# Loading order, weight pieces and paired start-up steps in an attention plus SmeLU kernel

## The chip, the cores and the metric

The kernel runs on one core of a Trainium2 chip. The metric is device time in microseconds. Before the change it is 308.18 us, the median of three runs (307.83 to 308.30). The profiled run took 307.91 us, and its trace spans 306.1 us from the first to the last instruction. A core has a matrix engine (PE, with its weight load PEld), a vector engine (DVE), a scalar engine (ACT), a GpSimd engine (POOL), and a SyncE engine (SP). Sixteen DMA engines move the data. POOL here mainly issues loads, [...].

## The reference: what is computed

```python
# attention: 8 batches, 8 heads, 576 positions, head size 64
scores = q @ k.T / sqrt(64)              # kept only where |i - j| <= 32
attn   = softmax(scores)
x      = (attn @ v)  ->  [8*576 = 4608 tokens, 8*64 = 512 features]
# feed-forward block
h = x @ w_in                             # w_in: 512 x 2048
g = h        if h >= 1                   # SmeLU with beta = 1
    0        if h <= -1
    (h+1)**2 / 4   otherwise
out = g @ w_out                          # w_out: 2048 x 512
```

All inputs and the output are float32 in DRAM. The kernel computes with bfloat16 operands and float32 sums.

## The kernel before

The work on the tokens goes in blocks of 256 (`TB`). For each block there are eight slots, one for each 256 of the 2048 hidden columns: `a = 8*t + f`. A slot projects (`project`: eight matmuls of 256 columns, two halves `j` by four 128-row groups `kk` of `w_in`), applies SmeLU, and leaves its result in `gT`. The products with `w_out` follow some slots later (`pair` for the first 512 tokens, `unit` after that). The attention of the next batch is spread between the slots. For the first batch there is nothing to hide it behind, so the start of the kernel is a hand-written prelude, and then slots 0 to 5 with the rest of batch 0's attention between them.

The order of the loads on POOL at the start (q of the first half goes by SP and ACT):

```python
def load_w_in(c0, c1, h):            # 64 partitions, 4 row groups, c1 - c0 columns
    nc.gpsimd.dma_start(out=w_in[64 * h:64 * h + 64, :, c0:c1],
                        in_=moe_w_in.rearrange("(h y d) f -> h d y f", h=2, d=64)[h][:, :, c0:c1])

# k of the first half (2 loads) ... then
load_v(0, 0)
P.affine_select(out=step, ...)       # for the identity and the mask
for n in range(1, 4):
    load_v(0, n)
...
cuts = [0, 256, 512, 768, 1024, 1280, 1792, DFF]
w = [(load_w_in, c0, c1, h) for c0, c1 in zip(cuts, cuts[1:]) for h in range(2)]
put(w[:4] + [(load_half, 1, t, h) for t in range(2) for h in range(2)] + w[4:12])   # load_half: rest of q, k
put([(load_w_out, 0, 0, 4)] + w[12:])
put([(load_w_out, 0, k, k + 4) for k in range(4, 16, 4)] + [(load_rows, 1, t) for t in range(2)])
put([(load_v, 1, n) for n in range(4)])
```

The prelude ends with the sums of the first 256 tokens (`sums` multiplies the exponentials with v and with ones; its `end` runs Ln and Exp on ACT, and `flush` later multiplies on DVE into `xT`). Then the rest of batch 0 hangs on slots 1 to 5:

```python
    scores(0, (1, 2), (0, 2), (0, 2), None, ps_p)
    keep_warm(4, ps_h, "hp")         # matmuls on zeros
    e0 = sums(0, 0, 0, TB)
    e1 = sums(0, 1, 0, TB, ps_p)
    keep_warm(5, ps_h, "hp")
    e0()
    e1()
# ...
pairs = [(6, 0), (7, 1), (8, 2), (9, 3), (11, 4), ...]          # (slot, pair of w_out)
two_on_act = (1, 7, 8, 9, 10, 11, 12)
at(1, (tposes, 0, (0, 1), (1, 1)))                               # rest of q and k transposed
at(2, (scores, 0, (0, 1), (0, 2), (2, 4)), (scores8, 0, ps_o))
at(3, (scores, 0, (1, 2), (0, 2), (2, 4), ps_n), (sums, 0, 0, TB, MAIN, ps_s))
at(4, (sums, 0, 1, TB, MAIN))
at(5, (sums, 0, 0, MAIN, S, ps_s))
```

In the slot loop (cut to what the change touches):

```python
for a in range(NF * NB + 2 * NF):
    # ...
    if a in (0,):                     # slots 0 and 1 are projected together
        hps = [ps_h.tile([128, 2, TB], FP, name="hp", tag="hp") for _ in range(2)]
        for y in range(2):
            for n in range(2):
                project(hps[n], f + n, r0, [(j, y + 2 * m) for j in range(2) for m in range(2)], y == 0, y == 1)
    elif not hps:
        # ps_o for slot 6, else ps_h
        hps = [pool.tile([128, 2, TB], FP, name="hp", tag=tag)]
        project(hps[0], f, r0, [(j, kk) for j in range(2) for kk in (0, 2, 1, 3)], True, True)
    hp = hps.pop(0)
    rr = ewp.tile([128, 2, TB], FP, name="rr")
    A.activation(rr, hp, AF.Relu, scale=0.5, bias=0.5)
    mx = ewp.tile([128, 2, TB], FP, name="mx")
    if a in two_on_act:
        A.activation(mx, rr, AF.Square)
        V.scalar_tensor_tensor(g, hp, 1.0, mx, op0=ALU.max, op1=ALU.min)
    else:
        V.tensor_max(mx, hp, rr)
        V.scalar_tensor_tensor(g, rr, 1.0, mx, op0=ALU.min, op1=ALU.mult)
    flush(); run(a)                  # the attention that hangs on this slot
    for x in post: ...               # pair or unit: products with w_out
```

Of the kernel before, what the change touches and what calls it, by code (L numbers as in the profile page):

```python
# [7 lines left out]
FP = mybir.dt.float32  # L8
# [6 lines left out]
def kernel(  # L15
# [30 lines left out]
    LONG = 2  # L46

# [7 lines left out]
    ps_h = ctx.enter_context(tc.tile_pool(name="ps_h", bufs=2, space=bass.MemoryType.PSUM))  # L55
# [25 lines left out]
    def load_half(half, t, h, eng=None, x=None):  # L81

        src, dst, nm = ((q, qn, "qh"), (k, kn, "kh"))[t]
        if (0, half) not in dst:
            dst[0, half] = early.tile([128, 2, S], BF, name=nm, tag=nm, bufs=2) if x is None else x
        (eng or nc.gpsimd).dma_start(out=dst[0, half][:, h], in_=src[0].rearrange(  # L86
            "(h y) (l p j) d -> h l p y (j d)", h=2, l=2, p=32)[h][half])
# [22 lines left out]
    def load_w_in(c0, c1, h):  # L110
        nc.gpsimd.dma_start(out=w_in[64 * h:64 * h + 64, :, c0:c1],  # L111
                            in_=moe_w_in.rearrange("(h y d) f -> h d y f", h=2, d=64)[h][:, :, c0:c1])
# [19 lines left out]
    load_v(0, 0)  # L132
    P.affine_select(out=step, in_=step, compare_op=ALU.is_ge, fill=-1.0, base=-65, channel_multiplier=-1,
                    pattern=[[1, 257]])
    for n in range(1, 4):
        load_v(0, n)
# [7 lines left out]
    def put(todo):  # L144
        for fn, *x in todo:
            fn(*x)

    cuts = [0, 256, 512, 768, 1024, 1280, 1792, DFF]
    w = [(load_w_in, c0, c1, h) for c0, c1 in zip(cuts, cuts[1:]) for h in range(2)]
    put(w[:4] + [(load_half, 1, t, h) for t in range(2) for h in range(2)] + w[4:12])  # L150
    put([(load_w_out, 0, 0, 4)] + w[12:])
    put([(load_w_out, 0, k, k + 4) for k in range(4, 16, 4)] + [(load_rows, 1, t) for t in range(2)])
# [60 lines left out]
    def scores(b, ys, pars, cs, eng, pool=ps_s, w=128, ready=None):  # L213

        if b not in pt:
            pt[b] = ptp.tile([128, 2, 2, 2, 512], BF, name="pt")
        ps = ready or two_banks(pool)
        n = 0
        if eng is None and not ready:
            cols = (ys[1] - ys[0]) * (pars[1] - pars[0]) * (cs[1] - cs[0])  # L220
            add_mask([ps[:, h] for h in range(2)], cols, w)
        for y1 in range(*ys):
            for par in range(*pars):
                for c2 in range(*cs):
                    c = 2 * c2 + par
                    for a in range(2):
                        for h in range(2):
                            s0 = S * (y1 + 2 * a) + 64 * c
                            nc.tensor.matmul(ps[HD[a], h, w * n:w * n + w], kT[b][HD[h], s0:s0 + 64],  # L229
                                             qTs[b % 3][HD[h], PAD + s0 - 32:PAD + s0 - 32 + w],  # L230
                                             start=eng is not None, stop=True, skip_group_check=True)
                    n += 1
        p = pt[b][:, :, ys[0]:ys[1], pars[0]:pars[1], 128 * cs[0]:128 * cs[1] - 128 + w]
        m = 2 if n > cs[1] - cs[0] else 1
        p = p[:, :, ys[0] - ys[0]] if ys[1] - ys[0] == 1 else p[:, :, :, 0]
        like = "p h (y j) -> p h y j"
        A.activation(p, ps[:, :, :w * n].rearrange(like, y=m), AF.Exp, scale=D ** -0.5)  # L237
        mask(eng, p, mask4[:, :256 * n].rearrange("p (h j) -> p h j", h=2).rearrange(like, y=m))

    def scores8(b, eng, pool=None):  # L240

        p = pt8[b] = ptp.tile([128, 2, 2, TAIL], BF, name="pt8")
        if pool:
            ps = [pool.tile([128, 2 * TAIL], FP, name="s8", tag="op") for h in range(2)]
        else:
            bb = two_banks(ps_s)
            ps = [bb[:, h, :2 * TAIL] for h in range(2)]
# [9 lines left out]
        like = "p h y j -> p h (y j)"  # L257
        if pool:
            for h in range(2):
                A.activation(p[:, h].rearrange("p y j -> p (y j)"), ps[h], AF.Exp, scale=D ** -0.5)  # L260
        else:
            A.activation(p.rearrange(like), bb[:, :, :2 * TAIL], AF.Exp, scale=D ** -0.5)
# [4 lines left out]
    def sums(b, y1, lo, hi, pool=ps_n):  # L267
# [3 lines left out]
        todo = []  # L271
        if lo < MAIN:
            ys, D0 = (y1,), w
            for par in range(2):
                a0 = max(lo, 32 * par)
                off = 32 - 64 * par
                todo.append((None, a0 - lo, hi - lo, lambda a, h, par=par, a0=a0, off=off: (
                    pt[b][HD[a], h, y1, par, a0 + off:hi + off])))
                for c2 in range(4):
                    q0, q1 = max(0, 128 * c2 - off, lo), min(128 * c2 + 128 - off, hi)  # L280
                    if q0 < q1:
                        todo.append((NC * y1 + 2 * c2 + par, q0 - lo, q1 - lo, lambda a, h, par=par, q0=q0, q1=q1, off=off: (
                            pt[b][HD[a], h, y1, par, q0 + off:q1 + off])))
# [36 lines left out]
    def tp1(pool):  # L320
        if pool is ps_h:
            return pool.tile([128, 8, 128], BF, name="tp", tag="hp")
        return pool.tile([128, 2, 8, 128], BF, name="tp", tag="bb")[:, 0]

    def tposes(b, *sets):

        todo = []
        for (t, half), pool in zip(sets, (ps_s, ps_n)):
            tp = pool.tile([128, 2, 8, 128], BF, name="tp", tag="bb")
# [4 lines left out]
    def keep_warm(n, pool, tag):  # L334

        z = pool.tile([128, 512], FP, name="z", tag=tag)
        for _ in range(n):
            nc.tensor.matmul(z, warm[:, :128], warm, start=True, stop=True)
# [9 lines left out]
    with tc.tile_pool(name="ps_p", bufs=1, space=bass.MemoryType.PSUM) as ps_p:  # L348
        keep_warm(11, ps_h, "hp")
# [6 lines left out]
        qq = [tpose(0, n, 0, (A.copy, V.tensor_copy)[n], tp1(ps_h)) for n in range(2)]  # L356
        for x in qq:
            x()
        kk = [tpose(0, n, 1, (A.copy, V.tensor_copy)[n], tp1((ps_n, ps_p)[n])) for n in range(2)]
        keep_warm(1, ps_h, "hp")  # L360
# [5 lines left out]
        scores(0, (0, 2), (0, 1), (2, 3), None, ps_n, 32)  # L366
        scores(0, (1, 2), (0, 2), (0, 2), None, ps_p)
        keep_warm(4, ps_h, "hp")
        e0 = sums(0, 0, 0, TB)
        e1 = sums(0, 1, 0, TB, ps_p)  # L370
        keep_warm(5, ps_h, "hp")
        e0()
        e1()
    ps_o = ctx.enter_context(tc.tile_pool(name="ps_o", bufs=2, space=bass.MemoryType.PSUM))

# [3 lines left out]
    pairs = [(6, 0), (7, 1), (8, 2), (9, 3), (11, 4), (12, 5), (15, 6), (15, 8), (16, 7), (17, 9)]  # L381
    two_on_act = (1, 7, 8, 9, 10, 11, 12)
# [13 lines left out]

    at(1, (tposes, 0, (0, 1), (1, 1)))
    at(2, (scores, 0, (0, 1), (0, 2), (2, 4)), (scores8, 0, ps_o))
    at(3, (scores, 0, (1, 2), (0, 2), (2, 4), ps_n), (sums, 0, 0, TB, MAIN, ps_s))
    at(4, (sums, 0, 1, TB, MAIN))  # L400
    at(5, (sums, 0, 0, MAIN, S, ps_s))
# [29 lines left out]
    def unit(x):  # L431

        tt, j = divmod(x, 16)
        if tt == NT // 128 - 1:
            half, n = divmod(j, 8)
            if n == 0:
                op[tt] = ps_o.tile([128, 256], FP, name="op", tag="op")
# [9 lines left out]
        if j == 0:  # L447
            op[tt] = ps_o.tile([128, DM], FP, name="op", tag="op")
# [7 lines left out]
    def pair(x):  # L456

        half, p, g = x // 8, x % 8 // 4, x % 4
        if (half, p) not in op:
            op[half, p] = ps_o.tile([128, 2, 256], FP, name="op", tag="op"), []  # L460
# [12 lines left out]
    def run(pos):  # L473
        todo = []
        for fn, *x in ev.get(pos, []):
# [4 lines left out]
            else:  # L480
                pool = (x.pop(),) if x[-1] in (ps_s, ps_n, ps_o) else ()
# [11 lines left out]
    hps = []  # L493
    done = 4 * (40 - NF)
    for a in range(NF * NB + 2 * NF):
# [9 lines left out]
        if a == 0 or a > 3:  # L505
            flush()
        if a < NF * NB:
            if wide:
# [3 lines left out]
                hp = ps_h.tile([128, 2, TB], FP, name="hp", tag="hp")  # L512
                for n, kk in enumerate((0, 2, 1, 3)):
# [3 lines left out]
            else:  # L517
                t, f = divmod(a, NF)
                r0 = TB * t % RING
                if a in (0,):  # L520
                    hps = [ps_h.tile([128, 2, TB], FP, name="hp", tag="hp") for _ in range(2)]
                    for y in range(2):
                        for n in range(2):
                            project(hps[n], f + n, r0, [(j, y + 2 * m) for j in range(2) for m in range(2)], y == 0, y == 1)
                elif not hps:
                    pool, tag = (ps_o, "op") if a == 6 else (ps_h, "hp")
                    hps = [pool.tile([128, 2, TB], FP, name="hp", tag=tag)]
                    project(hps[0], f, r0, [(j, kk) for j in range(2) for kk in (0, 2, 1, 3)], True, True)
                hp = hps.pop(0)
                g = gT[:, 2 * f:2 * f + 2, home(t)]  # L530

            rr = ewp.tile([128, 2, TB], FP, name="rr")
            A.activation(rr, hp, AF.Relu, scale=0.5, bias=0.5)  # L533
            mx = ewp.tile([128, 2, TB], FP, name="mx")
            if a in two_on_act:
                A.activation(mx, rr, AF.Square)
                V.scalar_tensor_tensor(g, hp, 1.0, mx, op0=ALU.max, op1=ALU.min)
            else:
                V.tensor_max(mx, hp, rr)  # L539
                V.scalar_tensor_tensor(g, rr, 1.0, mx, op0=ALU.min, op1=ALU.mult)  # L540
# [46 lines left out]
```

The softmax here doesn't subtract the row's maximum and nothing guards it: scores larger than these inputs give would overflow.

## Time and profile before

| engine | busy us | share of 306.1 us | instructions |
|---|---|---|---|
| PE | 298.4 | 97% | 3388 |
| DVE | 239.6 | 78% | 376 |
| ACT | 191.2 | 62% | 320 |
| POOL | 77.1 | 25% | 92 |

The chain of work that ended last is 91% PE, 3% POOL and 2% DMA. Some durations that matter later: a 512-column Relu on ACT takes 595 ns on average, `tensor_max` over 512 columns on DVE 689 ns, `scalar_tensor_tensor` 692 ns, a 1024-column Exp on ACT about 1.0 us. Eight matmuls of 256 columns that follow each other without a gap take 0.87 us on PE.

How to read it: a time line gives start, length, engine, source line, operation, tiles, and how many instructions were merged. What stands in brackets at its end is the idle time just before, with what ended it. Because PE is busy almost without a break, the end moves only if PE starts its dense work earlier or later, or if gaps in it open or close.

### The profile page before, as it was taken

How to read it: one execution, taken by the hardware profiler on the slowest of the kernel's cores; microseconds unless marked ns; L12 is line 12 of the kernel's file. 1: busy time of each engine (PE TensorE's matmuls, PEld its weight loads, DVE VectorE, ACT ScalarE, POOL GpSimd, SP SyncE). 2: the span in 40 equal slices, each digit the busy share in tenths (PEclk: the TensorE clock that was granted, in tenths of full speed). 3: DMA queues.
4: the chain of work that ended last, by engine and by line, in shares of the span. 5: the costliest groups of instructions: out<-in, count | busy, mean ns of one | idle time of the engine just before them, and what ended most of it. 6: DMA issues, size and time to landing. Idle time of an engine off the chain costs nothing.

```text
span 306.1 us, 7974 instructions
## 1 busy us (share of the span) xinstructions
PE 298.4 (97%) x3388; PEld 181.2 (59%) x3388; DVE 239.6 (78%) x376; ACT 191.2 (62%) x320; POOL 77.1 (25%) x92
## 2 busy tenths in 40 slices
PE   8889999999999999999999999999999999999995
PEld 3468878876666676666654544444445444446644
DVE  3268568888888989998999998888888888788700
ACT  3688896748856856776766766665667654444311
POOL 8787661037009009004600900000000000000000
PEclk9999999999999999999999999999999999999999
DMA  9999999999999999999998991550101000000121
GB/s 153 184 197 198 186 196 153 173 156 164 139 186 109 181 169 124 165 144 116 148 127 166 145 156 39 111 115 34 36 34 37 36 34 35 36 34 34 59 80 69
DMA packets 137171, 35.67 MB, mean 117 GB/s; under 512 B 122160, under 2 KB 132912, under 8 KB 137136
## 3 DMA queue, kind: packets, MB, share of 16 engines
q0 software_dynamic: 102976, 18.06, 83.5%
q1 hardware_dynamic: 34016, 16.81, 26.1%
q8 instruction: 26, 0.43, 0.6%
q10 hardware_dynamic: 144, 0.29, 0.3%
q14 instruction: 9, 0.07, 0.1%
HBM read 36.70 MB, written 9.44 MB: 151 GB/s over the span
## 4 chain that ended last, share of the span: by engine, by line
PE 91%; POOL 3%; DMA 2%; ACT 1%; issue 1%; DVE 0%; POOLq 0%; ACTq 0%
PE op L449 36%; PE hp L489 22%; PE hp L514 18%; PE bb L295 6%; PE op L464 4%; PE bb L229 2%; DMA w_in<-in_moe_w_in_dram 2%; POOL vn L107 1%; PE op L440 1%; POOL w_in L111 1%; PE tp L189 1%; ACT pt L237 1%; POOL kh L86 1%; POOL qh L86 0%; PE bb L208 0%
## 5 line engine op out<-in xcount | busy, mean ns | idle before, releaser
L533 ACT ACTIVATE rr<-hp 128x512 f32<-128x512 f32 x144 | 85.5, 595 | 86.1 <-PE hp L514 41.7
L449 PE MATMUL op<-w_out,gT 128*128 128x512 bf16 x496 | 126.9, 380 | 0.0
L539 DVE TENSOR_TENSOR mx<-hp,rr 128x512 f32<-128x512 f32 x137 | 94.4, 689 | 26.1 <-ACT rr L533 24.3
L540 DVE SCALAR_TENSOR_TENSOR gT<-rr,mx 128x512 bf16<-128x512 f32 x137 | 94.8, 692 | 4.7
L489 PE MATMUL hp<-xT,w_in 128*128 128x256 bf16 x640 | 83.1, 273 | 2.2 <-DMA w_in<-in_moe_w_in_dram 1.4
L489 PEld LDWEIGHTS <-w_in 128*128 128x128 bf16 x640 | 61.8, 98 | 22.7 <-issue 2.8
L449 PEld LDWEIGHTS <-gT 128*128 128x128 bf16 x496 | 46.1, 98 | 45.2
L514 PE MATMUL hp<-xT,w_in 128*128 128x512 bf16 x256 | 65.7, 379 | 0.0
L514 PEld LDWEIGHTS <-w_in 128*128 128x128 bf16 x256 | 25.0, 98 | 30.2
L99 POOL DMA_DIRECT2D qn<-in_q_dram x12 | 14.6, 1224 | 89.5 <-DMA kT<-kn 87.4
L237 ACT ACTIVATE pt<-bb 128x1024 bf16<-128x1024 f32 (+1 forms) x33 | 32.7, 1001 | 4.5 <-PE bb L229 3.1
L107 POOL DMA_DIRECT2D vn<-in_v_dram x32 | 27.7, 900 | 4.8 <-DMA w_out<-in_moe_w_out_dram 4.0
L307 DVE TENSOR_TENSOR xT<-bb,rc 128x512 bf16<-128x512 f32 (+1 forms) x32 | 21.0, 657 | 9.6 <-ACT rc L302 8.7
L453 ACT COPY osb<-op 128x512 f32<-128x512 f32 x31 | 18.0, 580 | 11.4 <-PE op L449 11.1
L302 ACT ACTIVATE rc<-lr 128x512 f32<-128x512 f32 (+2 forms) x40 | 23.5, 587 | 1.3
L301 ACT ACTIVATE lr<-bb 128x512 f32<-128x512 f32 (+2 forms) x40 | 22.1, 552 | 0.3 <-PE bb L295 0.3
L203 DVE TENSOR_TENSOR pt<-pt,mask 128x1024 bf16<-128x1024 bf16 (+1 forms) x33 | 20.3, 614 | 0.5 <-ACT pt L237 0.5
L295 PE MATMUL bb<-pt,ones 64*64 64x256 bf16 (+3 forms) x352 | 19.6, 255 | 0.1
L295 PE MATMUL bb<-pt,vn 64*64 64x128 bf16 (+3 forms) x712 | 18.4, 204 | 0.1
L295 PEld LDWEIGHTS <-ones 64*64 64x64 bf16 x352 | 10.3, 105 | 11.6 <-issue 11.6
L295 PEld LDWEIGHTS <-vn 64*64 64x64 bf16 x712 | 16.7, 107 | 0.3 <-DMA vn<-in_v_dram 0.3
L464 PE MATMUL op<-w_out,gT 128*128 128x256 bf16 x128 | 16.5, 273 | 0.0
(61 smaller groups left out, 140.3 us busy)
## 6 DMA issues: line engine op xcount, KB each, us to landing
out_dram<-osb SPq DMA_DIRECT2D x35, 256.0 KB, 2.3
vn<-in_v_dram POOLq DMA_DIRECT2D x32, 144.0 KB, 9.7
qn<-in_q_dram POOLq DMA_DIRECT2D x12, 288.0 KB, 6.2
kn<-in_k_dram POOLq DMA_DIRECT2D x12, 288.0 KB, 9.0
w_in<-in_moe_w_in_dram POOLq DMA_DIRECT2D x12, 128.0 KB, 5.6
w_out<-in_moe_w_out_dram POOLq DMA_DIRECT2D x4, 256.0 KB, 8.0
w_out<-in_moe_w_out_dram POOLq DMA_DIRECT2D x2, 512.0 KB, 13.2
kh<-in_k_dram POOLq DMA_DIRECT2D x4, 144.0 KB, 5.4
```

The costliest lines, as they stand in the source:

```text
L107: nc.gpsimd.dma_start(out=vn[b][64 * a:64 * a + 64, :, h], in_=v[b, y:y + 2].rearrange("y s d -> (y s) d") .rearrange("(c r) d -> r c d", ...
L237: A.activation(p, ps[:, :, :w * n].rearrange(like, y=m), AF.Exp, scale=D ** -0.5)
L295: nc.tensor.matmul(bb[HD[h], a, o + c0:o + c1], ones[HD[a]] if c is None else vn[b][HD[a], c, h], p(a, h), start=n == 0, stop=True, skip_g ...
L301: A.activation(lr[:, :, :D0], bb[:, :, D0:2 * D0], AF.Ln)
L302: A.activation(rc[:, :, :D0], lr[:, :, :D0], AF.Exp, scale=-1.0)
L449: nc.tensor.matmul(op[tt], gT[:, j, home(tt // 2), 128 * (tt % 2):128 * (tt % 2) + 128], w_out[:, j], start=j == 0, stop=j == 15)
L464: nc.tensor.matmul(o[:, tt], gT[:, j, p, 128 * tt:128 * tt + 128], w_out[:, j, 256 * half:256 * half + 256], start=not done, stop=len(done ...
L489: nc.tensor.matmul(hp[:, j], w_in[:, kk, 256 * f + 128 * j:256 * f + 128 * j + 128], xT[:, kk, r0:r0 + TB], start=first and n == 0, stop=l ...
L514: nc.tensor.matmul(hp.rearrange("p n t -> p (n t)"), w_in[:, kk, 128 * f:128 * f + 128], xT[:, kk, r0:r0 + 2 * TB], start=n == 0, stop=n == 3)
L533: A.activation(rr, hp, AF.Relu, scale=0.5, bias=0.5)
L539: V.tensor_max(mx, hp, rr)
L540: V.scalar_tensor_tensor(g, rr, 1.0, mx, op0=ALU.min, op1=ALU.mult)
```

## The change

It has four parts.

1. The rest of batch 0's q and k (four loads) is issued ahead of v, and before the first weights.
2. `w_in` is loaded in sixteen pieces of one row group (128 partitions) by 512 columns, in place of fourteen pieces of 64 partitions, four row groups and 256 or 512 columns. The first `w_out` piece goes behind all of `w_in`.
3. All scores of the rest of batch 0 but one set, and the last tail scores, move into the prelude. Slots 0 to 5 are done two at a time (`double`), so that Relu, max and the last step take 1024 columns in one instruction. The remaining sums of batch 0 lie between these doubles.
4. PSUM is laid out anew: the two banks for projections and the two for output are one tile each, and the code picks the bank. `rr` and `mx` have four places instead of three. The exponentials of a 32-column edge get a small tile of their own (`pb`). Pairs 0 to 3 sit one slot later.

It is meant to let the first batch's attention finish early, and to let the projections begin as each row group arrives. The core of the diff, with cuts marked:

```diff
+    KK = 0, 2, 1, 3
...
-    def load_w_in(c0, c1, h):
-        nc.gpsimd.dma_start(out=w_in[64 * h:64 * h + 64, :, c0:c1],
-                            in_=moe_w_in.rearrange("(h y d) f -> h d y f", h=2, d=64)[h][:, :, c0:c1])
+    def load_w_in(c0, c1, kk):
+        nc.gpsimd.dma_start(out=w_in[:, kk, c0:c1],
+                            in_=moe_w_in.rearrange("(h y d) f -> y h d f", h=2, d=64)[kk][:, :, c0:c1])
...
-    load_v(0, 0)
+    load_half(1, 0, 0)
     P.affine_select(out=step, ...)
-    for n in range(1, 4):
+    for t, h in ((0, 1), (1, 0), (1, 1)):
+        load_half(1, t, h)
+    for n in range(4):
         load_v(0, n)
...
-    put(w[:4] + [(load_half, 1, t, h) for t in range(2) for h in range(2)] + w[4:12])
-    put([(load_w_out, 0, 0, 4)] + w[12:])
-    put([(load_w_out, 0, k, k + 4) for k in range(4, 16, 4)] + [(load_rows, 1, t) for t in range(2)])
+    put([(load_w_in, c, c + 512, kk) for c in range(0, DFF, 512) for kk in KK])
+    put([(load_w_out, 0, k, k + 4) for k in range(0, 16, 4)] + [(load_rows, 1, t) for t in range(2)])
...
         scores(0, (1, 2), (0, 2), (0, 2), None, ps_p)
-        keep_warm(4, ps_h, "hp")
+        tp = tp2(ps_e)
+        qq = [tpose(0, 2 + n, 0, V.tensor_copy, tp[:, n]) for n in range(2)]
+        ...                                    # the same for k, three warm matmuls
+        scores(0, (0, 1), (0, 2), (2, 4), None, ready=rest)
         e0 = sums(0, 0, 0, TB)
         e1 = sums(0, 1, 0, TB, ps_p)
-        keep_warm(5, ps_h, "hp")
         e0()
+        flush()
         e1()
+        flush()
+        scores8(0, None)
+        keep_warm(4, ps_e)
...
-    pairs = [(6, 0), (7, 1), (8, 2), (9, 3), (11, 4), ...]
-    two_on_act = (1, 7, 8, 9, 10, 11, 12)
+    pairs = [(7, 0), (8, 1), (9, 2), (10, 3), (11, 4), ...]
+    two_on_act = (7, 8, 9, 10, 11, 12)
...
+    rrs, mxs = (ewp.tile([128, 4, 2, TB], FP, name=nm, bufs=1) for nm in ("rr", "mx"))
+    def smelu(hp, g, a, n): ...               # as before, over n slots at once, flush() after Relu
+
+    def double(n, between):
+        hp = (hps, ops.rearrange("p n (j t) -> p n j t", j=2))[n % 2]
+        for kk in KK:
+            for f in range(2):
+                project(hp[:, f], 2 * n + f, 0, [(j, kk) for j in range(2)], kk == KK[0], kk == KK[-1])
+            if kk == KK[1]:
+                between()
+        smelu(hp.rearrange("p n j t -> p (n j) t"), gT[:, 4 * n:4 * n + 4, home(0)], 2 * n, 2)
+
+    double(0, lambda: scores(0, (1, 2), (0, 2), (2, 4), None, ps_n))
+    sums(0, 0, TB, MAIN, ps_s)()
+    double(1, lambda: None)
+    sums(0, 1, TB, MAIN)()
+    double(2, lambda: sums(0, 0, MAIN, S, ps_s)())
-    for a in range(NF * NB + 2 * NF):
+    for a in range(6, NF * NB + 2 * NF):
```

## The prediction

> **What bounds the kernel now.** I read the page first: PE is busy 97% of the span, so only the start can move much. Then the time line of PE over the first 35 us:
>
> ```profile
> 13.24 0.60 PE L489 MATMUL hp<-xT,w_in 128*128 128x256 bf16 x4 [0.44 <-DVE xT L307]
> 14.50 1.47 PE L489 MATMUL hp<-xT,w_in 128*128 128x256 bf16 x12 [0.67 <-DMA w_in<-in_moe_w_in_dram]
> ...
> 18.53 1.03 PE L489 MATMUL hp<-xT,w_in 128*128 128x256 bf16 x8 [0.72 <-DMA w_in<-in_moe_w_in_dram]
> ...
> 25.23 1.05 PE L489 MATMUL hp<-xT,w_in 128*128 128x256 bf16 x8
> 26.11 1.04 PE L464 MATMUL op<-w_out,gT 128*128 128x256 bf16 x8
> ...
> 33.59 1.03 PE L489 MATMUL hp<-xT,w_in 128*128 128x256 bf16 x8 [0.33 <-DVE gT L537]
> ```
>
> Up to 18.53 us PE waits for weights again and again. From there it runs densely, apart from one gap that ends at 33.59 us. Slot 6 is the group at 25.23. By then all attention of batch 0 is done; after the change it is done there too, and behind slot 6 both kernels hold the same work. So slot 6 is my mark: how much earlier or later it runs is how much the end moves.
>
> What feeds it is the DMA, as a chart of its rate over 0 to 12 us (0.3 us a slice) and a table over later stretches (last column GB/s) show:
>
> ```profile
> GB/s 0 0 0 0 0 0 0 200 223 276 361 361 407 238 215 142 134 142 175 169 154 156 154 155 157 152 145 125 131 144 155 165 174 187 198 186 201 190 196 191
> ```
>
> ```profile
> 12.00:15.00 3.00, 1.89 (x13) 1.04 (x12) 1.38 (x2) 1.69 (x3) 1.62 (x4) 1.00 1.26 204
> 18.00:21.00 3.00, 2.47 (x47) 1.98 (x48) 2.19 (x5) 2.00 (x3) 2.89 (x5) 1.00 1.35 200
> 21.00:24.00 3.00, 2.92 (x89) 2.15 (x87) 2.03 (x3) 2.97 (x7) 2.08 (x4) 1.00 1.35 192
> ```
>
> These are bytes written: about 150 GB/s while v comes in (runs of 64 elements), 195 to 200 otherwise. The loads write bfloat16 from float32, so some 390 GB/s are read. The DMA is the bound from 2 us on. Third, POOL's time line:
>
> ```profile
> 14.65 1.83 POOL L111 DMA_DIRECT2D w_in<-in_moe_w_in_dram x3 [1.28 <-DMA w_in<-in_moe_w_in_dram]
> ...
> 22.74 0.74 POOL L93 DMA_DIRECT2D qn<-in_q_dram x1 [0.42 <-DMA w_in<-in_moe_w_in_dram]
> 23.99 0.74 POOL L93 DMA_DIRECT2D kn<-in_k_dram x1 [0.50 <-DMA w_in<-in_moe_w_in_dram]
> 25.46 2.55 POOL L107 DMA_DIRECT2D vn<-in_v_dram x3 [0.73 <-DMA w_out<-in_moe_w_out_dram]
> ```
>
> POOL waits here for loads to land, though nobody overwrites their tiles. Counting POOL's loads in program order, these are numbers 18, 29, 30 and 31, and what they wait for fits 10, 21, 22 and 23: always eight back. So at most eight POOL loads are in flight. It also tells when loads landed: number 22 just before 23.99, number 23 just before 25.46.
>
> [...]
> [...]
> [...] The trace: 390 GB/s read over 16 engines are 24.4 each.
> [...] The trace: ACT's 288 KB q load lands 3.2 us after its issue.
> [...] the eleven 512-column warm matmuls at the start take 4.88 us, 0.44 each, and later ones of that size follow at 0.22.
>
> **The change, part by part.**
>
> *Moving q and k ahead of v and weights.* Bytes before v: first-half q 0.59 MB, first-half k 0.295, the rest of q and k 0.59. The rate chart sums to 0.68 MB at 5.1 us; the other 0.79 MB at 200 GB/s end at 9.0; v, 0.59 MB at 150, at 13.0 (10.3 before). Transposes, scores and Exps of the second half fit into this wait, some 4 us of PE that costs nothing. Sums follow at about 13.3, and with Ln, Exp and the multiply (0.60 + 0.63 + 0.69, from ACT and DVE at 11.2 to 13.2) xT is there at 15 to 17.
>
> *w_in by row groups.* A piece is 128 partitions by 512 columns, 131 KB written. The rows of one group are 64 and 64, with 192 between (heads y and y+4), so the source's slowest dimension counts 2. [...] The total rate is the same, but one piece now takes long: [...] (before, one of these sizes took 0.67 us of all engines). Pieces 1 to 4 (columns 0 to 511) move from 13.0 to 18.4 and land near 19.3. Pieces 5 to 8 are issued when v's loads land, 12 to 14.5, and land near 20 to 22. Piece 9 can't be issued until piece 1, eight before it, has landed: 19.3. Then come eight issues of 0.6 us (L111: 0.62), the last ending at 24.1, [...]: pieces 9 to 12 land by about 28.5, and piece 16 at 31.1 to 31.5.
> Slot 6 uses columns 1536 on and needs piece 16 in its fourth matmul; three of 0.11 us lie before it. Its effective start is 31.3 - 0.3 = 31.0 against 25.23: **+5.8 us**. Nothing fills the wait, since the attention is done and the w_out products come after.
>
> *Doubles.* One 1024-column DVE step replaces two of 0.69; from 0.55, 0.62 and 0.69 us for 384, 448 and 512 columns the slope is 0.0011 us a column, so 1.25 for 1024. Six such steps save 0.8 us of DVE, and Relu some 0.2 each on ACT. Double 2's chain, arriving at 29, ends on DVE near 34.6 (Relu 1.0, two pending multiplies 1.2, then 2 x 1.25); slot 8 needs the bank after the max, 33.4, and comes at 33.6 (slots 6, 7 and pair 0 at 0.87 each). Tight, but **0**.
>
> *Pairs one slot later.* The gap before slot 11 (33.10 to 33.59) came from slots 10 and 11 running without a pair between. Now pair 3 lies there: **-0.4 us**. w_out's first piece, number 27, waits for number 19, is issued at 27 to 28 and lands near 32: pair 0 at 32.7 has it.
>
> *PSUM tiles and rr/mx places*: still two banks in turn for projections and two for output; **0**.
>
> *Clock.* PE is now idle about 3 us before double 0 and 3 us before double 2. If the clock falls to half and the dense part starts with it, [...] I give it one chance in three: **+0.5**.
>
> Sum: 5.8 - 0.4 + 0.5 = 5.9. I take off 0.3, [...]: 308.2 + 5.6 = **313.8 us**.
>
> **Rivals.**
> (A) [...] Then only the bytes count, and they are easily compared: up to its last w_in piece the new order moves 4.16 MB (q 0.59, k 0.295, rest 0.59, v 0.59, weights 2.10), just what the old one moved up to number 23 (w_out's first piece in place of two w_in units), which landed at 25.4. Slot 6 then starts at 25.1, 0.1 earlier, and with the closed gap the kernel takes about 307.7. For it speaks that all loads so far run at full rate[...]. I give it 13%.
> (B) [...] the clock stays cold for longer, or loads from numbers 27 on (w_out, then q and k of batch 1) come late and PE starves again at slots 8 to 11: 315 to 317. Against it: [...] batch 1's q and k are used only at slot 11, some 8 us after slot 6.
> (C) The DVE line binds, as three doubles with a multiply each need 3.1 us of DVE in a row; [...] and slot 8 would wait a few tenths: 308. At the slow pace it has time.
>
> **Range and chances.** The main line gives 311 to 316.5 by the moment pieces land (plus or minus 1 us)[...] and the clock (0 to 2); rival A puts a small island at 307 to 308.5 outside. The range is 310.8 to 316.4. The 2% line is 314.34, a bit above my middle: slower by over 2% 0.38, within 2% 0.61 (A included), faster 0.01.
>
> **What would show it.** In the new trace: w_in loads with 7 to 9 us from issue to landing where 5.6 was the median; a POOL wait of several us ahead of the ninth piece; PE idle before double 2 and up to about 31 us, ended by w_in; slot 6 near 31. DMA rate well under 195 GB/s at 20 to 30 us. If the pieces land 0.65 us apart with slot 6 near 25, [...] A is right. If double 2's PE group takes 0.2 us a matmul, the clock fell. If slots 6 to 11 show DVE waits, C took part.

## The result, and the profile after

The changed kernel takes 415.75 us (median of four runs, 415.2 to 416.6) against 308.24 us before, a ratio of 1.348 (95% interval 1.344 to 1.353). I had predicted 313.8.

The page of the changed kernel shows at once that this is no matter of the start alone. The lines are the span, the busy time of PE and ACT, and the shares of the chain that ended last:

```profile
span 413.9 us, 7977 instructions
PE 324.1 (78%) x3394; PEld 183.2 (44%) x3394; DVE 243.2 (59%) x372; ACT 190.8 (46%) x314; POOL 81.0 (20%) x94
PE 41%; ACT 25%; DVE 21%; DMA 7%; issue 4%; POOL 1%; ACTq 0%; POOLq 0%
```

PE ran almost the same number of instructions (3394, before 3388), but its share fell from 97% to 78%, and the chain, 91% PE before, now goes through ACT and DVE for almost half of its length. No engine is full. The list of waits (engine, line, what it waited for, then us in total, times, longest) has new entries:

```profile
PE hp L505 <- DVE mx L520: 28.6, 44, 1.4
PE hp L557 <- DVE mx L520: 28.1, 46, 1.3
PE op L465 <- ACT osb L469: 12.0, 14, 2.2
```

A projection waits for DVE's max, and a product with `w_out` for ACT's copy. Which max? The chain in order of time tells (start, length, what; slots 17 and 18 of the changed kernel):

```profile
69.98 1.05 PE hp L505 x8
...
71.05 0.61 ACT rr L514
...
71.68 0.70 DVE mx L520
...
72.42 1.03 PE hp L505 x8
```

The next projection starts right after the max of the slot just before it, though that max reads the other bank. A slot is now a row of 1.05 + 0.61 + 0.70 us and small gaps: the two projections start 72.42 - 69.98 = 2.44 us apart. In the kernel before, the same two slots, with the same pair between them, started 50.56 - 48.81 = 1.75 us apart:

```profile
48.81 1.04 PE L489 MATMUL hp<-xT,w_in 128*128 128x256 bf16 x8
49.68 1.04 PE L464 MATMUL op<-w_out,gT 128*128 128x256 bf16 x8
50.56 1.04 PE L489 MATMUL hp<-xT,w_in 128*128 128x256 bf16 x8
```

The time after my mark says how much this is: from the end of slot 6 to the end of the kernel it was 306.1 - 26.3 = 279.8 us, and now, with slot 6 ending at 36.4, 413.9 - 36.4 = 377.5. So 97.7 us come from behind slot 6, and 10.1 from ahead of it. The three waits listed add up to 68.7 us; PE's own busy time also grew, from 298.4 to 324.1 us.

For the part ahead, this is PE's time line after the change, beside the one that the prediction shows of before:

```profile
25.36 0.78 PE L505 MATMUL op<-xT,w_in 128*128 128x256 bf16 x4 [1.51 <-DMA w_in<-in_moe_w_in_dram]
...
28.98 1.89 PE L505 MATMUL hp<-xT,w_in 128*128 128x256 bf16 x8 [1.92 <-DMA w_in<-in_moe_w_in_dram]
...
35.50 0.89 PE L505 MATMUL op<-xT,w_in 128*128 128x256 bf16 x5 [0.88 <-DMA w_in<-in_moe_w_in_dram]
37.79 1.86 PE L505 MATMUL op<-xT,w_in 128*128 128x256 bf16 x8 [1.41 <-DVE mx L520]
41.73 1.87 PE L480 MATMUL op<-w_out,gT 128*128 128x256 bf16 x8 [2.07 <-DVE gT L518]
```

The group at 35.50 is the rest of slot 6, held up by the last piece of `w_in`. Slot 7 at 37.79 waits for the max of slot 6 although it has the other output bank. Eight matmuls of 256 columns take 1.86 us there, twice the 0.87 of before: PE is at half clock, which the table by stretch shows too (after the stretch and its length come the busy times of PE, PEld, DVE, ACT and POOL, then the granted clock, 0.50, the DMA share and GB/s):

```profile
38.00:44.00 6.00, 3.93 (x19) 2.60 (x18) 1.16 (x2) 1.23 (x2) 4.43 (x7) 0.50 1.28 205
```

POOL's time line fits eight loads in flight, as predicted, with each `w_in` piece waiting for the load eight back:

```profile
15.11 0.78 POOL L111 DMA_DIRECT2D w_in<-in_moe_w_in_dram x1 [0.29 <-DMA vn<-in_v_dram]
18.75 1.57 POOL L111 DMA_DIRECT2D w_in<-in_moe_w_in_dram x2 [2.87 <-DMA w_in<-in_moe_w_in_dram]
...
25.60 0.78 POOL L111 DMA_DIRECT2D w_in<-in_moe_w_in_dram x1 [1.08 <-DMA w_in<-in_moe_w_in_dram]
29.22 2.34 POOL L116 DMA_DIRECT2D w_out<-in_moe_w_out_dram x3 [2.84 <-DMA w_in<-in_moe_w_in_dram]
```

PE's waits place the landings a little more sharply: piece 1 by 18.5 (PE loads its weights then), piece 8 (issued at 15.11) by 25.4, piece 9 by 29.0 and piece 16 (issued at 25.60) by 35.5. The page's median from issue to landing, before and after, and the stretch from 21 to 24 us after the change (57 GB/s, where the kernel before moved 192) say the same:

```profile
w_in<-in_moe_w_in_dram POOLq DMA_DIRECT2D x12, 128.0 KB, 5.6
w_in<-in_moe_w_in_dram POOLq DMA_DIRECT2D x16, 128.0 KB, 9.9
21.00:24.00 3.00, 2.57 (x43) 1.39 (x40) 1.60 (x2) 2.34 (x4) 3.00 (x5) 1.00 0.98 57
```

### The profile page after: what moved, and what is told of

Its sections match the earlier page's. It is cut to its first block, busy times and chain, and to the rows that moved or that the text cites. A ratio compares the mean times of both kernels' runs of the same rounds, so it can differ in the third digit from the quotient of the medians.

```text
span 413.9 us, 7977 instructions
## 1 busy us (share of the span) xinstructions
PE 324.1 (78%) x3394; PEld 183.2 (44%) x3394; DVE 243.2 (59%) x372; ACT 190.8 (46%) x314; POOL 81.0 (20%) x94
## 2 busy tenths in 40 slices
DMA packets 150003, 35.73 MB, mean 86 GB/s; under 512 B 136528, under 2 KB 145744, under 8 KB 149968
## 4 chain that ended last, share of the span: by engine, by line
PE 41%; ACT 25%; DVE 21%; DMA 7%; issue 4%; POOL 1%; ACTq 0%; POOLq 0%
DVE mx L520 16%; PE hp L505 14%; PE hp L557 13%; ACT rr L514 12%; ACT pt L239 5%; PE op L465 5%; DMA w_in<-in_moe_w_in_dram 5%; PE bb L296 4%; DVE xT L308 3%; ACT rc L303 2%; ACT lr L302 2%; ACT osb L469 2%; DMA vn<-in_v_dram 2%; PE op L480 2%; PE bb L228 1%
## 5 line engine op out<-in xcount | busy, mean ns | idle before, releaser
L514 ACT ACTIVATE rr<-hp 128x512 f32<-128x512 f32 (+1 forms) x138 | 82.9, 601 | 173.5 <-PE hp L505 91.1
L520 DVE TENSOR_TENSOR mx<-hp,rr 128x512 f32<-128x512 f32 (+1 forms) x133 | 92.8, 698 | 107.5 <-ACT rr L514 107.2
L465 PE MATMUL op<-w_out,gT 128*128 128x512 bf16 x496 | 128.4, 379 | 12.0 <-ACT osb L469 12.0
L505 PE MATMUL hp<-xT,w_in 128*128 128x256 bf16 x608 | 81.0, 277 | 33.8 <-DVE mx L520 28.6
L521 DVE SCALAR_TENSOR_TENSOR gT<-rr,mx 128x512 bf16<-128x512 f32 (+1 forms) x135 | 95.0, 704 | 4.6
L239 ACT ACTIVATE pt<-bb 128x1024 bf16<-128x1024 f32 x32 | 32.7, 1024 | 8.1 <-PE bb L228 6.1
L308 DVE TENSOR_TENSOR xT<-bb,rc 128x512 bf16<-128x512 f32 (+1 forms) x32 | 21.0, 657 | 10.2 <-ACT rc L303 9.9
L480 PE MATMUL op<-w_out,gT 128*128 128x256 bf16 x128 | 17.8, 287 | 2.1 <-DVE gT L518 2.1
L296 PEld LDWEIGHTS <-vn 64*64 64x64 bf16 x712 | 17.6, 111 | 1.1 <-DMA vn<-in_v_dram 1.1
```

Source lines behind the costliest of these rows:

```text
L296: nc.tensor.matmul(bb[HD[h], a, o + c0:o + c1], ones[HD[a]] if c is None else vn[b][HD[a], c, h], p(a, h), start=n == 0, stop=True, skip_g ...
L308: muls.append(lambda: V.tensor_mul(o, bb[:, :, :D0], rc[:, :, :D0]))
L465: nc.tensor.matmul(op[tt], gT[:, j, home(tt // 2), 128 * (tt % 2):128 * (tt % 2) + 128], w_out[:, j], start=j == 0, stop=j == 15)
L505: nc.tensor.matmul(hp[:, j], w_in[:, kk, 256 * f + 128 * j:256 * f + 128 * j + 128], xT[:, kk, r0:r0 + TB], start=first and n == 0, stop=l ...
```

## The experiments

Theory T: an engine's instruction waits for the other engines' instructions on the same PSUM tile, whichever bank they touch. Rival B (another one than the prediction's B): waits go by bank, and something else in the new layout (the common rr and mx tiles, rival R) does it. Theory K: the smaller the outermost count of a piece's source pattern, the longer the piece takes to land; at the time of the prediction this was my assumption, which the trace of the kernel before did not show. Rival A: only bytes count. Theory D came up on the way.

### One part of the PSUM layout at a time, in the kernel before

**e1**, the two projection banks as one tile, taken in the same turn, from slot 0 on (the prelude keeps two tiles of its own); nothing else:

```diff
-    hp = ps_h.tile([128, 2, TB], FP, name="hp", tag="hp")     # pool with bufs=2
+    hp = hp2[:, turn_h[0] % 2]                                # hp2: one tile [128, 2, 2, TB]
```

> The kernel before, with nothing changed but the two projection banks: one tile of two banks, picked in turn, in place of two tiles of one bank. Theory T (an engine waits for the others on any part of one PSUM tile, whichever bank): each slot becomes projection 1.0, Relu 0.61, max 0.70 us in a row, 2.3 to 2.6 us where it was 1.75, over some 130 slots: 385 to 405 us, and PE waits for DVE's max for 50 us or more in the profile. Rival R (the common rr and mx tiles bring the waits): 308. Rival B (waits go by bank): 308.

Measured: 400.25 us, ratio 1.297 (1.295 to 1.300). Its waits:

```profile
PE hp L497 <- DVE mx L546: 35.7, 48, 1.7
PE hp L522 <- DVE mx L546: 31.3, 49, 1.3
```

The kernel before lists no such waits. Instructions, their order and the number of banks are the same; only the object that the banks belong to differs, and it costs 92 us, of which 67.0 are these two waits and 19.1 are PE's busy time (317.5 us against 298.4). So the waits go by tile. T holds, B falls. The runs show the waits that the program has, not whether the chip would need them.

**e2**, the same with the two output banks (`op_bank()`, as in the change):

> The kernel before, with only the two output banks made one tile. T: PE's first product of each 128 tokens waits for ACT's copy of the 128 before, 32 times, 0.4 to 0.9 us each: 318 to 335 us. R and B: 308.

Measured: 328.87 us, ratio 1.066 (1.063 to 1.069), with PE waiting 12.2 us in 14 places for ACT's copy (I had expected 32 places). T again, though this wait is less than the 20 us lost.

**e3**, rr and mx as one SBUF tile each:

```diff
-    rr = ewp.tile([128, 2, TB], FP, name="rr")
+    rr = rrs[:, a % 4]                                        # rrs: one tile of four places; mx likewise
```

> The kernel before, with only rr and mx made one tile each with four places. T: no change, 307.5 to 309. R: if writes and reads of neighbouring places in one SBUF tile wait for each other, ACT's Relu waits for DVE of the slot before: 380 or more.

Measured: 308.40 us, ratio 1.000 (0.999 to 1.001). Rival R falls: places in one SBUF tile don't hold each other up here. It is a matter of the PSUM tiles.

**e4**, the changed kernel with its two-bank tiles kept for the doubles only, and two one-bank tiles each for projections and output in the slot loop, slots 6 and 7 included:

```diff
+    dd.close()                                                # the doubles' two-bank tiles end here
+    ps_h = ctx.enter_context(tc.tile_pool(name="ps_h", bufs=2, space=bass.MemoryType.PSUM))
+    ps_o = ctx.enter_context(tc.tile_pool(name="ps_o", bufs=2, space=bass.MemoryType.PSUM))
     ...
-    hp = hps[:, a % 2]
+    hp = ps_h.tile([128, 2, TB], FP, name="hp", tag="hp")     # output likewise, from ps_o
```

> The kernel after, with the doubles on two-bank tiles as they are, but from slot 8 on two tiles of one bank each for projections and for output, as before. T: what is left is the late weights (slot 6 some 10 us late), the slots 6 and 7 and the cold clock: 316 to 324 us. R: still 400 or more.

Measured: 318.42 us, ratio 1.032 (1.030 to 1.034). Of the 107.5 us lost, this undoes 97.3. What is left, 10.2 us, is the start.

### How w_in's pieces are spread

Three kernels, each the one before with only the pieces of `w_in` changed: always sixteen pieces of 128 partitions by 512 columns, in the old order of loads. Only the rows that a piece gathers differ.

```diff
-    in_=moe_w_in.rearrange("(h y d) f -> h d y f", h=2, d=64)[h][:, :, c0:c1]     # before: 64 partitions x 4
+    in_=moe_w_in.rearrange("(h y d) f -> y h d f", h=2, d=64)[kk][:, :, c0:c1]    # e5: 2 x 64 rows, as in the change
+    in_=moe_w_in.rearrange("(h y d) f -> y h d f", h=4, d=32)[kk][:, :, c0:c1]    # e6: 4 x 32 rows
+    in_=moe_w_in.rearrange("(y d) f -> y d f", d=128)[kk][:, c0:c1]               # e7: 128 rows
```

> The kernel before, with only w_in's pieces changed to those of the change (one row group of 64 + 64 rows by 512 columns, sixteen pieces, in the old order of loads). Theory K [...]: 9 to 10.5 us from issue to landing for w_in, where 5.6 was the median; with eight loads in flight the last piece lands at 38 to 41 us: 318 to 326 us. Rival A (bytes alone count): 307.5 to 310.

> As e5, but each piece gathers four blocks of 32 rows, so that the outermost count is 4 (other rows of w_in than the reference's reach each group, so the output differs; sizes and number of pieces are those of e5). K: [...] landing 6 to 7.5 us after issue: 310 to 316. A, or a loss from the gap between the rows as such: as e5.

> As e5, but each piece takes 128 rows that follow each other, so that the outermost count is 128 (again other rows than the reference's, same sizes and pieces). K: [...] 4.6 to 6.5 us from issue to landing: 307 to 309.5. A rival that blames pieces of one row group, or their number: as e5.

Measured: e5 322.24 us, ratio 1.045 (1.042 to 1.049); e6 314.11, ratio 1.019 (1.017 to 1.021); e7 310.74, ratio 1.007 (1.005 to 1.008). e6 and e7 compute with other rows of `w_in`; their loads have the sizes of e5's. The DMA view of each gives packets of the whole run (each "under" includes the smaller ones), and loads with size and median us from issue to landing. e5:

```profile
DMA packets 150003, 35.73 MB, mean 111 GB/s; under 512 B 136528, under 2 KB 145744, under 8 KB 149968
w_in<-in_moe_w_in_dram POOLq DMA_DIRECT2D x16, 128.0 KB, 9.0
```

e6:

```profile
DMA packets 141811, 35.69 MB, mean 114 GB/s; under 512 B 128336, under 2 KB 137552, under 8 KB 141776
w_in<-in_moe_w_in_dram POOLq DMA_DIRECT2D x16, 128.0 KB, 6.7
```

e7:

```profile
DMA packets 135667, 35.67 MB, mean 115 GB/s; under 512 B 122192, under 2 KB 131408, under 8 KB 135632
w_in<-in_moe_w_in_dram POOLq DMA_DIRECT2D x16, 128.0 KB, 5.6
```

Landing goes 9.0, 6.7, 5.6 us with the outermost count 2, 4, 128. That is the order that K asks for, with the same bytes in the same number of pieces, and A falls; so does a loss from the gaps between the rows as such, for e6 has more gaps than e5. The traces show times and packets, not which engine carried what, so why the count matters is not shown.

The packets show something else that I had not counted. e5 has 150003 - 135667 = 14336 more than e7, and e6 has 6144 more. The rows themselves aren't cut up: the packets from 512 B to 2 KB are 9216 in all three (145744 - 136528 in e5), and in the trace of the changed kernel, which loads the same pieces as e5, 2048 packets of POOL's queue have 1024 bytes, one for each row of the sixteen pieces. The additional ones are 0.06 MB in all in e5, some 4 bytes each; the changed kernel's trace has 15712 packets of 4 bytes in POOL's queue, the one of before 1344. Per piece they are 896 in e5 and 384 in e6. The runs don't show what these packets are for.

The pieces also moved more slowly than I had assumed. From 15 to 18 us the changed kernel moved 151 GB/s, and 162 from 17 to 18, with all of pieces 1 to 8 issued; e8 below moved 199 and 200 in these stretches (I had assumed 195). Whether the small packets cause this, no run tells.

e7's own loss of 2.5 us, above its expected range, I can't settle. In its profile slot 2 waits three times for `w_in` (0.36, 0.44 and 0.35 us) where before it waited once (0.72), and PE has one gap of 1.80 us near 26 us that ends on nothing the profile shows. The profiled run took 312.68 us, the longest of the five, so the gap may be of that run alone.

### What is left when both are undone

**e8**, e4 with `w_in` in sixteen pieces of outermost count 64:

```diff
-    nc.gpsimd.dma_start(out=w_in[:, kk, c0:c1], in_=...("(h y d) f -> y h d f")[kk][:, :, c0:c1])
+    y, h = divmod(n, 2)
+    nc.gpsimd.dma_start(out=w_in[64 * h:64 * h + 64, y::2, c0:c1],
+                        in_=...("(h y d) f -> h d y f")[h][:, y::2, c0:c1])
```

> The kernel after with both faults undone: separate tiles of one bank from slot 8 on, and w_in in sixteen pieces of 64 partitions, two row groups and 512 columns (same bytes, outermost count 64). T and K together: the last piece lands near 25.4, slot 6 near 25, no cold clock: 307 to 309.5. If something else in the change costs too: 312 or more.

Measured: 311.89 us, ratio 1.010 (1.007 to 1.014). This gives 6.5 us back against e4, but 3.6 us remain: something else costs too. Slots 6 and 7 now run at 26.01, 0.8 later than slot 6 ran before, and then (PE's and DVE's time lines of e8):

```profile
26.01 1.91 PE L505 MATMUL op<-xT,w_in 128*128 128x256 bf16 x16
31.09 1.86 PE L480 MATMUL op<-w_out,gT 128*128 128x256 bf16 x8 [3.17 <-DVE mx L520]
32.75 1.91 PE L505 MATMUL hp<-xT,w_in 128*128 128x256 bf16 x8
```

```profile
27.96 1.22 DVE L520 TENSOR_TENSOR mx<-hp,rr 128x1024 f32<-128x1024 f32 x1
29.21 1.23 DVE L521 SCALAR_TENSOR_TENSOR gT<-rr,mx 128x1024 bf16<-128x1024 f32 x1
30.36 0.68 DVE L520 TENSOR_TENSOR mx<-op,rr 128x512 f32<-128x512 f32 x1
```

Pair 0 needs the output bank that slot 6 used, and slot 6's max, at 30.36, stands behind three doubles and three multiplies that have kept DVE busy without a break since 21.6. After this wait of 3.17 us pair 0 and slot 8 run at half clock, 1.86 and 1.91 us for eight matmuls. In the table by stretch PE does nothing from 28 to 31 us, and the granted clock is 0.52 after that:

```profile
28.00:31.00 3.00, 0.00 (x0) 0.00 (x0) 2.97 (x4) 1.19 (x2) 1.82 (x4) 1.00 1.42 199
31.00:34.50 3.50, 3.41 (x17) 2.43 (x17) 1.99 (x3) 0.00 (x0) 3.50 (x4) 0.52 1.21 207
```

This is theory D. It is a real wait for one bank and no fault of the tiles.

**e9**, e8 with pairs 0 to 3 on slots 9, 9, 10, 10 and slot 6's square on ACT, so that slots 8 and 9 fill the wait:

> e8 with the first pairs of w_out moved behind slots 8 and 9 (pairs 0 and 1 on slot 9, pairs 2 and 3 on slot 10) and slot 6's square on ACT. Theory D (what is left in e8 is DVE: three doubles and three multiplies stand in a row from 21.6 us on, and pair 0 waits 3.2 us for the output bank that slot 6's max still reads): slot 8 runs at 29.3 instead of 32.8 and the clock does not fall: 308.5 to 309.8 us. Rival (late weights, or the loads of batch 1, hold the slots anyway): 311 to 312, as e8.

Measured: 309.81 us, ratio 1.006 (1.004 to 1.008). Slots 8 and 9 run at 28.98 at full pace (sixteen matmuls in 1.91 us, where eight took that long in e8), as D says; by the medians 2.1 us come back, with runs that scatter by about as much (e8 310.8 to 313.2, e9 309.5 to 311.5). The result is at the upper edge of what I expected, and still 1.4 us behind the kernel before. Part of that is DVE again: slots 8 and 9 wait 1.31 us for the max of the last double:

```profile
28.98 1.91 PE L505 MATMUL hp<-xT,w_in 128*128 128x256 bf16 x16 [1.31 <-DVE mx L520]
```

### Two parts alone, in the kernel before

**e10**, only `pairs = [(7, 0), (8, 1), (9, 2), (10, 3), ...]`:

> The kernel before with only pairs 0 to 3 one slot later. The prediction's term: the gap before slot 11 closes, -0.3 to -0.5 us, 307.7 to 308.0. Rival: the slots 6 and 7 without a pair between open a gap of their own, 308.2 or more.

Measured: 308.15 us beside 308.45, ratio 0.9995 (0.9986 to 1.0003), no difference that can be told. The gap before slot 11 did close in its profile, but slot 5 waited 0.58 us for `w_in` there, so that profile doesn't show where the gain went.

**e11**, only the order of loads (q and k ahead of v and the first weights):

```diff
-    load_v(0, 0)
+    load_half(1, 0, 0)        # the other three behind affine_select, then load_v(0, 0..3), then w[:12]
```

> The kernel before with only the rest of batch 0's q and k loaded ahead of v and the first weights; slots, tiles and w_in's pieces as before. By bytes v lands 2.7 us later and the first weights 2.9 us later, but then the transposes need no wait of their own: slots 0 and 1 at 17.3, PE 1.9 us behind at slot 2: 309.5 to 311. If DVE, which then starts its SmeLU steps 3 us later, becomes the bound as in e8: 311 to 313. If the order costs nothing: 308.2.

Measured: 312.22 us, ratio 1.012 (1.010 to 1.013): this part alone costs 3.8 us. PE's time line of e11:

```profile
13.41 0.29 PE L297 MATMUL bb<-pt,vn 64*64 64x96 bf16 x2 [1.61 <-DMA vn<-in_v_dram]
15.14 0.39 PE L297 MATMUL bb<-pt,vn 64*64 64x96 bf16 x8 [1.44 <-DMA vn<-in_v_dram]
...
18.82 2.16 PE L491 MATMUL hp<-xT,w_in 128*128 128x256 bf16 x16
```

v lands at 15.1, not at 13.0 as the bytes say. After the wait PE is at half clock (0.29 us of work from 12 to 15 us, then a granted clock of 0.50 from 15 to 18, in which the sums run), and slots 0 and 1 start at 18.82, where I had 17.3. In this profile, of a run of 312.7 us, slot 2 runs at 22.04, 3.5 us later than before. Slot 3, at 25.03, is 4.8 us later, because PE first waits 0.82 and 0.20 us for DVE's copies of the transposed q and k:

```profile
23.91 0.41 PE L210 MATMUL bb<-bias,ident 64*64 64x512 bf16 x4 [0.82 <-DVE qT L194]
24.52 0.42 PE L231 MATMUL bb<-qT,kT 64*64 64x128 bf16 x16 [0.20 <-DVE kT L194]
```

DVE has no break from 21.21 to 25.76 us there. So most of the loss is v's late landing and the clock, and a smaller part is DVE, the second branch of the expectation, in whose range the result lies.

No version beat the kernel before by more than the scatter.

## Why the prediction was wrong

*PSUM tiles.* "still two banks in turn for projections and two for output; **0**." This is the step that failed, and it is 97 of the 107 us (e4): I had put its cost at nothing. I had asked which banks an instruction touches. The waits go by the tile, and with one tile there is one chain PE, ACT, DVE, PE in place of two that overlap (e1, e2). The rr and mx half of that step was right (e3).

*w_in by row groups.* That these pieces land late was my assumption, and the landing times of e5 to e7 bear it out (9.0, 6.7 and 5.6 us). The course of it was right: eight in flight, the ninth piece after the first, PE idle before double 2 and up to the last piece. The time of one piece was mis-sized. From the end of the last issue (24.1) to the last landing (31.1 to 31.5) I had 7.0 to 7.4 us, an estimate of mine; the median from issue to landing is 9.9. The rate was lower than I had assumed (151 and 162 GB/s for 195); how much of the difference that makes is not shown. Piece 1 landed by 18.5 (19.3 predicted), but piece 8 by 25.4 (20 to 22) and the last by 35.5 (31.3), since it could be issued only when piece 8 had landed. Slot 6's effective start is 35.50 - 0.33 = 35.2, so the term is +9.9 us, not +5.8. Rival A had no part in it.

*Clock.* I gave it one chance in three, +0.5 us. It happened: a granted clock of 0.50 at 38 to 44 us in the changed kernel. In e4, where the tiles don't hide it, slot 7 and pair 0 run at about half pace: 13 matmuls take 2.61 us and the next eight 1.73, where eight in a row took 0.87 before. From the first of the 13, at 35.40, to slot 8, at 39.37, these 21 take 3.97 us, and at 0.87 for eight they would take 2.28, so I estimate a loss of some 1.7 us. In e8 the granted clock was 0.52 after a gap of 3.17 us.

*Doubles.* The length of a 1024-column step was right (1.21 to 1.23 us in e8, 1.25 predicted). "**0**" held at the slow pace, as DVE had time (in e4, slot 6's max starts within a microsecond of its Relu). With the pieces of e8, which land in 5.7 us by the median, rival C, which I had put at a few tenths and at slot 8, is a wait of 3.17 us at pair 0 plus the half clock after it (e8, granted 0.52), and with the pairs moved away still 1.31 us at slot 8 (e9). I had followed the projection banks and not the output banks.

*Moving q and k.* The sum has no term for it, and alone it costs 3.8 us (e11): v lands 2 us later than its bytes say, PE's granted clock is 0.50 after the wait, and DVE comes late with its copies. The reading of the chart was off too: it sums to 0.77 MB at 5.1 us, not 0.68, which would put v 0.4 us earlier, not later. In the changed kernel the late weights seem to hide this; no run separates the two there.

*Pairs.* -0.4 us can't be told from nothing (e10: between -0.4 and +0.1).

## What to carry to other kernels

Give each PSUM bank that is to run in turn with another its own tile; in these runs two banks in one tile were one resource as far as waits go, even where the code picked the bank (e1 lost 92 us, e2 20). Before regrouping a load, look at the outermost count of its source pattern, then at packets and time to landing in the DMA view: the same bytes in the same number of pieces took 5.6 us with count 128 (e7) and 9.0 with count 2 (e5). And before making work start later in larger lumps, lay out the engine that has to drain it, bank by bank: in e8 DVE had no break from 21.6 us on until slot 6's max at 30.36, PE stood for 3.17 us, and its granted clock was 0.52 after that.

## What the runs showed of the hardware that I had not expected

A casting load of 128 rows with outermost count 2 or 4 came with 896 or 384 packets of some 4 bytes beside its 128 rows of 1 KB, which stayed whole, more than with count 128 (e5 and e6 against e7); issuing a piece took POOL 0.84 and 0.67 us against 0.53 (medians in e5, e6, e7). The runs don't show why.

PE fell to half clock more than once in one kernel, each time after a stretch of low busy time, though it was not idle throughout. The changed kernel was granted 0.57 from 15 to 18 us (1.02 us of work in the 3 us before), 0.50 from 27 to 30 (1.64 before, at a granted clock of 0.78), and 0.50 from 36 to 44 (1.19 before).
